# Reordering the start of the second attention of a two-layer decode kernel on Trainium2

## The chip, the cores and the metric

The kernel runs on one core of a Trainium2 chip. The metric is the device time of one execution in microseconds (us), median of several runs. All times inside an execution are counted from the start of the profiled span.

## The reference

```python
def _A_ref(x, k_cache, v_cache, wq, wo):            # x: 4 x 1 x 512, caches: 4 x 8 x 8192 x 128
    W = 2048                                        # the last 2048 rows of the caches
    q = (x @ wq) as 4 x 32 heads x 1 x 128
    k, v = last W rows, each of 8 KV heads serves 4 query heads
    p = softmax(q k^T * 128**-0.5)
    return (p v as 4 x 1 x 4096) @ wo
def _B_ref(x, w_gate, w_up, w_down):                # 512 -> 1792 -> 512
    return (sigmoid(x @ w_gate) * (x @ w_up)) @ w_down

x = x + _A_ref(layernorm(x)); x = x + _B_ref(layernorm(x))
x = x + _A_ref(layernorm(x)); x = x + _B_ref(layernorm(x))    # same weights and caches again
```

Everything is bf16 outside; there are four tokens (one per batch element), so every weight and every cache row is read for very little arithmetic.

## The kernel before

**One planner, five queues.** The Python functions below record operations with `P.op(engine, name, planned duration, emit, r=, w=, banks=)`. `_schedule` then orders each engine's operations by planned times; the order is fixed when the program is built, and each engine works through its list strictly in that order. Reads, writes and PSUM banks decide which semaphores an operation waits for. After the first layer `P.chain` is set: TensorE then follows the order in which the operations were recorded.

**Memory.** `arena` has 50 slots of 512 KB (a tile is two slots, 1 MB). Sixteen tiles hold K of all eight KV heads (`kpair(h, bp)`, two tiles for each head, `bp` picks two of the four batch elements); the rest circulate among wq, wo, V, gate, up and down. K is loaded once and stays, transposed in place, for the second attention. V is loaded twice, except that two V tiles are kept: one stays in the arena, the other is copied by VectorE into PSUM banks 0 to 3 at the end of the first attention (`stash`, operations `st0` to `st3`) and copied back in the second (`load_stash`, operations `us0` to `us3`, L517). The copies back may run once the first q of the second attention is turned (`fresh`).

**DMAs.** All weights and caches go through SyncE's queue at L398, in the order of the list `loads`. A load is recorded when a tile becomes free (`done` or `pool.release`, then `fill`); its DMA waits for the last reader of the tile's old content, and all later DMAs of the queue stand behind it.

**The second attention** (`attn_second`) works heads 7 to 0 as units 0 to 7. In each unit:

- `qx(u)`: TensorE spreads q (L721), ScalarE copies it to `qbd` (L726);
- `score(u)`: four mask matmuls (L751) and 16 score matmuls (L758) into one PSUM bank; then both K tiles of that head are released, which records the next V loads;
- `soft(u)`: on VectorE the maximum `mx` (L767), two copies (L771), `mk` (L775) and `nm` (L779); on ScalarE the exponential (L782), which writes `prow`;
- `turn(u)`: TensorE permutes `prow` (L795, PSUM bank 2), ScalarE copies it back (L797), VectorE transposes it to `ebuf` (L802);
- `sum_up(u)` (POOL L891, L898, L908; TensorE L903; VectorE L905), `pv_wide` (L925, then VectorE L933, L938, L940), and the output projection (L959, L965, L978). Unit 7 takes an older path (`pv_unit`, L844).

q comes in two halves. `q_second` makes the half for heads 4 to 7. The half for heads 0 to 3 is made inside `attn_second` from two wq tiles by `q_mms(1, 0, ...)` (L674), and turned by `q_turn` (VectorE L687, L691).

Before the change the recorded order at the top of `attn_second` is: spread q for unit 0; the first two quarters of the other q half; spread q for unit 1; score 0; score 1; softmax 0; turn 0; spread q for unit 2; the last two quarters of q; sums 0; turn of q; softmax 1. The stashed V returns to the tile that the first of those two wq tiles leaves.

**The last GLU** (`glu(1, 0, NB, True)`): gate matmuls and up matmuls (L1174, four chunks `c` each), VectorE transposes (L1183) and the gating (L1189 to L1201), then the down matmuls (L1214), which add to rows of x that `x_rows` (POOL L1149, TensorE L1156) has put into the same PSUM bank. ScalarE and VectorE copy the sum out (L1225) and SyncE stores it.

Of the kernel before, what the change touches and what calls it, by code (L numbers as in the profile page):

```python
# [278 lines left out]
def build(nc, A_x, A_k, A_v, A_wq, A_wo, B_wg, B_wu, B_wd, out, cfg=None):  # L279
    cfg = dict(cfg or {})  # L280
    tm = dict(_TM)
# [40 lines left out]
    with es:  # L322
# [188 lines left out]
        def load_stash(name):  # L511
            left[name] = 1

            def emit(s):
                for n, b in [(n, STASH[n]) for n in (1, 2, 3, 0)]:
                    dst = tile_ap(s)[:, n * 1024:(n + 1) * 1024].bitcast(F32)
                    o = P.op("vector", "us%d" % n, c_dve(512), lambda v, dst=dst, b=b: v.transpose(dst, ps[:, b, :]),  # L517
                             r=[("stash", n)], w=[("slot", s + n // 2)], banks=(b,))
                    o.deps.update(fresh)
            loads.append((name, emit))  # L520
# [219 lines left out]
        def softmax_unit(tag, hk, wait=False, q=True):  # L740
            u = ucount[0]
            ucount[0] += 1
            k2 = u % 2
            bank, pt = {HKV: (OBS[0], 2), HKV + 1: (WB, 3)}.get(u, (SB[k2], k2))
            if q:
                q_unit(tag, hk, k2)

            def e_s(pe):
                last = None
                for gi in range(4):  # L750
                    last = pe.matmul(ps[32 * gi:32 * gi + 32, bank, :], msk_s[:, :],  # L751
                                     msk_m[:, :].unsqueeze(1).broadcast_to([128, 256, 2]), start=True, stop=False)
                for cp in range(4):
                    for gi in range(4):
                        jh, bp = gi // 2, gi % 2
                        kt = kpair(hk, bp).rearrange("p (j c k t) -> p c t j k", c=2, k=32, t=2)
                        q0 = ((k2 * 4 + cp) * 2 + bp) * 32
                        last = pe.matmul(ps[32 * gi:32 * gi + 32, bank, :], qbd[:, q0:q0 + 32],  # L758
                                         kt[:, cp // 2, cp % 2, jh * NJ:(jh + 1) * NJ, :], start=False, stop=(cp == 3))
                return last  # L760
            P.op("tensor", "S" + tag, 20 * tm["pe_row"], e_s,
                 r=[("msk_s",), ("msk_m",)] + [("slot", 4 * hk + t) for t in range(4)] + [("q", k2)],
                 w=[("pss", pt)], banks=(bank,))
            def soft():
                mk = mxt[:, k2 * 32:(k2 + 1) * 32]
                P.op("vector", "mx" + tag, c_dve(512),
                     lambda v: v.tensor_reduce(nmax[:, k2:k2 + 1], ps[:, bank, :], AXX, ALU.max),  # L767
                     r=[("pss", pt)], w=[("mx", k2)], banks=(bank,))
                for g in range(2):
                    P.op("vector", "nx%d%s" % (g, tag), tm["dve_small"],  # L770
                         lambda v, g=g: v.tensor_copy(nmax[64 * g:64 * g + 64, 4 + k2:5 + k2],  # L771
                                                      nmax[64 - 64 * g:128 - 64 * g, k2:k2 + 1]),
                         r=[("mx", k2)], w=[("nx", k2, g)])
                P.op("vector", "mk" + tag, tm["dve_small"],
                     lambda v: v.scalar_tensor_tensor(mk, nmax[:, 4 + k2:5 + k2].broadcast_to([128, 32]), nmax[:, k2:k2 + 1],  # L775
                                                      maskr[:, :], ALU.max, ALU.add),
                     r=[("mx", k2), ("nx", k2, 0), ("nx", k2, 1), ("maskr",)], w=[("mk", k2)])
                P.op("vector", "nm" + tag, tm["dve_small"],
                     lambda v: v.tensor_reduce(nmax[:, 2 + k2:3 + k2], mk, AXX, ALU.max, negate=True, apply_transpose=True),  # L779
                     r=[("mk", k2)], w=[("nm", k2)])  # L780
                P.op("scalar", "ex" + tag, c_act(512) + 200.0,
                     lambda a: a.activation(prow[:, :].rearrange("p (m x t) -> p m x t", x=32, t=2),  # L782
                                            ps[:, bank, :].rearrange("p (m t x) -> p m x t", x=32, t=2), ACTF.Exp, bias=nmax[:, 2 + k2:3 + k2], scale=1.0,
                                            accum_out=psm[:, k2:k2 + 1]),
                     r=[("pss", pt)] + [("nm", k2)], w=[("prow",), ("psm", k2)], banks=(bank,))

            if wait:
                late[tag] = soft
            else:
                soft()  # L790
            return k2
# [260 lines left out]
        def attn_second():  # L1052
            hs = list(range(HKV))[::-1]

            def tag(u):
                return "2.%d" % u

            def turn(u):
                turn_p(2, tag(u), u % 2, PBS[0], u < NW)

            def qx(u):
                if u < HKV:
                    q_unit(tag(u), hs[u], u % 2)

            def score(u):
                if u >= HKV:
                    return
                softmax_unit(tag(u), hs[u], True, False)
                for bp in range(2):
                    pool.release(4 * hs[u] + 2 * bp)  # L1070
                fill()

            def soft(u):
                if u < HKV:
                    late.pop(tag(u))()

            def sum_up(u):
                if u < NW:
                    sums(tag(u), u % 2)
                elif u < HKV:  # L1080
                    sums_old(tag(u), u % 2)

            qx(0)
            q_mms(1, 0, OBS[1], (0, 1))
            qx(1)
            score(0)
            score(1)
            soft(0)
            turn(0)
            qx(2)  # L1090
            s = need(wq_part(1, NC - 1, 0)[0])
            left[wq_part(1, NC - 1, 0)[0]] += 1
            q_mms(1, 0, OBS[1], (2, 3))
            wide_buffers(s, P.ops[-1])
            sum_up(0)
            q_turn(1, 0, OBS[1], rest["tv", 1], [("tv", 1)], [o for o in P.ops if o.name == "pt2.0"])
            soft(1)
            op = {}

            def wo(u):  # L1100
                wo_wide(tag(u), hs[u], op[u], u % 2, u == 0, u == NW - 2)

            def back(u):
                op[u] = late.pop(("tr", tag(u)))()

            for u in range(NW):
                if u == NW - 1:
                    back(u - 1)
                    wo(u - 1)
                pv_wide(tag(u), hs[u], u % 2, v_tiles[(2, hs[u])])  # L1110
                turn(u + 1)
                if 0 < u < NW - 1:
                    back(u - 1)
                score(u + 2)
                soft(u + 2)
                if u == NW - 1:
                    wo_back()
                sum_up(u + 1)
                qx(u + 3)
                if 0 < u < NW - 1:  # L1120
                    wo(u - 1)
            u = NW

            def between():
                wo_compact(tag(u - 1), hs[u - 1], late.pop(("tr", tag(u - 1)))(), (u - 1) % 2)
            wo_unit(tag(u), hs[u], pv_unit(tag(u), hs[u], u % 2, v_tiles[(2, hs[u])], between), u % 2, False, True)
# [10 lines left out]
        def glu(k, b0, b1, last=False):  # L1137
# [24 lines left out]
            egv = eg[:, 0:NH].rearrange("p (k b) -> p k b", b=NB)  # L1162
            for n, nm in enumerate(("wg", "wu")):
                for c in range(NC):
                    if n and c == 2 and last:
                        x_rows()
                    name = (nm, c // 2, k)
                    s = need(name)

                    def e_g(pe, c=c, s=s, n=n):  # L1170
                        last = None
                        for g in range(4):
                            o = c % 2 * F + g * NF
                            last = pe.matmul(ps[32 * g:32 * g + NB, OBS[n], 0:NF], xn[:, c * NB:(c + 1) * NB],  # L1174
                                             tile_ap(s)[:, o:o + NF], start=(c == 0), stop=(c == NC - 1))
                        return last
                    P.op("tensor", "gl%s%d_%d" % (nm, k, c), 4 * tm["pe_row"], e_g,
                         r=tok(s) + [("xn",)], w=[("gu", n)], banks=(OBS[n],))
                    done(name)
# [7 lines left out]
                if n == 0:  # L1187
# [13 lines left out]
                 lambda v: v.tensor_tensor(hT[:, 0:NH].rearrange("p (k b) -> p k b", b=NB), tv, egv, ALU.mult),  # L1201
                 r=[("e", 0), ("e", 1), ("eg",), ("q", 0)], w=[("hT",)])
            if last:
                for (a, b) in bounds_of(k):
                    name = ("wd", a, k)
                    s = need(name)
# [157 lines left out]
```

## Time and profile before

| | us |
|---|---|
| median of 6 runs | 183.9 (183.42 to 184.71) |
| the profiled execution: its own time | 184.37 |
| the profiled execution: its span | 182.6 |
| TensorE busy | 100.2 (55%) |
| VectorE busy | 102.0 (56%) |
| ScalarE busy | 32.9 (18%) |
| POOL busy | 21.4 (12%) |
| SyncE's DMA queue: 71.84 MB, share of 16 engines | 96.4% |
| HBM read | 71.83 MB, 393 GB/s over the span |

Busy shares are averages over stages that differ: in the first attention VectorE transposes K, in the second it doesn't. The page's slices cut the span into 40 parts of 4.57 us. The second attention begins near 126 us and ends near 170 us, the last GLU after it.

### The profile page before, as it was taken

How to read it: one execution, taken by the hardware profiler on the slowest of the kernel's cores; microseconds unless marked ns; L12 is line 12 of the kernel's file. 1: busy time of each engine (PE TensorE's matmuls, PEld its weight loads, DVE VectorE, ACT ScalarE, POOL GpSimd, SP SyncE). 2: the span in 40 equal slices, each digit the busy share in tenths (PEclk: the TensorE clock that was granted, in tenths of full speed). 3: DMA queues.
4: the chain of work that ended last, by engine and by line, in shares of the span. 5: the costliest groups of instructions: out<-in, count | busy, mean ns of one | idle time of the engine just before them, and what ended most of it. 6: DMA issues, size and time to landing. Idle time of an engine off the chain costs nothing.

```text
span 182.6 us, 3840 instructions
## 1 busy us (share of the span) xinstructions
PE 100.2 (55%) x1627; PEld 54.1 (30%) x1639; DVE 102.0 (56%) x253; ACT 32.9 (18%) x87; POOL 21.4 (12%) x86
## 2 busy tenths in 40 slices
PE   1434425662816508254186566445866978757663
PEld 1002111342412504224146531321323333326331
DVE  6208997668384393744942633212978587743351
ACT  2002032121210202102002001001154244331011
POOL 7000010110010100101001000000024133322000
PEclk9999999999999999999999999999999699999555
DMA  5999999999999999999999999999999999999970
GB/s 198 420 425 429 425 414 417 422 420 414 418 416 425 423 422 413 422 416 423 407 423 418 410 402 414 357 371 387 416 357 414 427 427 418 423 406 408 412 312 16
DMA packets 12305, 72.09 MB, mean 395 GB/s; under 512 B 1144, under 2 KB 1152, under 8 KB 5632
## 3 DMA queue, kind: packets, MB, share of 16 engines
q1 hardware_dynamic: 12280, 71.84, 96.4%
q8 instruction: 13, 0.21, 0.5%
q14 instruction: 4, 0.03, 0.0%
q10 hardware_dynamic: 8, 0.00, 0.0%
HBM read 71.83 MB, written 0.00 MB: 393 GB/s over the span
## 4 chain that ended last, share of the span: by engine, by line
DMA 37%; DVE 27%; PE 23%; ACT 4%; SPq 3%; issue 3%; POOL 0%; DVEq 0%; ACTq 0%
DMA arena<-in_A_v_cache_dram 19%; DMA arena<-in_B_w_down_dram 12%; DVE arena L733 11%; PE ps L758 9%; DMA arena<-in_A_wq_dram 5%; PE ps L844 5%; DVE nmax L767 4%; SPq L398 3%; PE ps L751 3%; ACT prow L782 3%; DVE nmax L771 2%; DVE mxt L775 2%; DVE arena L933 1%; PE ps L1024 1%; DVE arena L517 1%
## 5 line engine op out<-in xcount | busy, mean ns | idle before, releaser
L733 DVE STREAM_TRANSPOSE arena<-arena 128x1024 f32<-128x1024 f32 x32 | 37.0, 1203 | 0.0
L758 PE MATMUL ps<-arena,qbd 128*32 128x512 bf16 x256 | 26.0, 541 | 0.0
L844 PE MATMUL ps<-ebuf,arena 128*128 128x8 bf16 x576 | 17.8, 168 | 9.4 <-DMA arena<-in_A_v_cache_dram 5.3
L767 DVE TENSOR_REDUCE nmax<-ps 128x1 f32<-128x512 f32 x16 | 11.0, 687 | 18.3 <-PE ps L758 18.3
L751 PE MATMUL ps<-msk_m,msk_s 128*32 128x512 bf16 x64 | 8.7, 532 | 22.0 <-DVE arena L733 21.8
L844 PEld LDWEIGHTS ps<-ebuf,arena 128*128 128x128 bf16 x576 | 16.8, 104 | 11.5 <-DMA arena<-in_A_v_cache_dram 6.4
L782 ACT ACTIVATE prow<-ps,nmax 128x512 bf16<-128x512 f32 x16 | 11.0, 687 | 37.5 <-DVE nmax L779 34.8
L726 ACT CAST qbd<-ps 128x256 bf16<-128x256 f32 x16 | 6.0, 373 | 47.1 <-PE ps L758 34.7
L674 PE MATMUL ps<-arena,xn 128*4 128x512 bf16 x64 | 7.9, 577 | 8.4 <-DMA arena<-in_A_wq_dram 7.3
L758 PEld LDWEIGHTS ps<-arena,qbd 128*32 128x32 bf16 x256 | 8.7, 123 | 10.4 <-issue 8.3
L811 POOL CAST s<-psm 128x1 bf16<-128x1 f32 x9 | 1.7, 189 | 84.5 <-ACT prow L782 84.0
L797 ACT CAST prow<-ps 128x512 bf16<-128x512 f32 x16 | 9.4, 586 | 10.8 <-PE ps L795 2.8
L802 DVE STREAM_TRANSPOSE ebuf<-prow 128x256 f32<-128x256 f32 x16 | 7.0, 439 | 4.7 <-ACT prow L797 4.6
L687 DVE STREAM_TRANSPOSE ebuf<-ps 128x512 f32<-128x512 f32 x3 | 2.2, 717 | 12.7 <-PE ps L674 12.6
L721 PE MATMUL ps<-qh,eyew 32*128 32x64 bf16 x64 | 5.7, 220 | 5.6 <-ACT qbd L726 2.4
L751 PEld LDWEIGHTS ps<-msk_m,msk_s 128*32 128x32 bf16 x64 | 1.8, 101 | 23.4 <-DVE arena L733 19.0
L655 ACT ACTIVATE lnv<-ps 128x4 f32<-128x4 f32 x4 | 0.7, 174 | 42.7 <-PE ps L651 42.7
L1174 PE MATMUL ps<-arena,xn 128*4 128x448 bf16 x64 | 7.0, 564 | 2.5 <-DMA arena<-in_B_w_up_dram 1.8
L852 DVE TENSOR_TENSOR onb<-ps,rinv 128x16 bf16<-128x16 f32 x9 | 1.7, 186 | 10.7 <-PE ps L844 10.7
L925 PE MATMUL ps<-arena,ebuf 128*32 128x512 bf16 x112 | 7.5, 389 | 0.0
L933 DVE STREAM_TRANSPOSE arena<-ps 128x512 f32<-128x512 f32 x7 | 5.0, 708 | 3.3 <-PE ps L925 3.3
L795 PEld LDWEIGHTS ps<-prow,perm 128*128 128x128 bf16 x16 | 1.6, 100 | 16.8 <-ACT prow L782 16.0
(105 smaller groups left out, 127.6 us busy)
## 6 DMA issues: line engine op xcount, KB each, us to landing
arena<-in_A_v_cache_dram SPq DMA_DIRECT2D x30, 1024.0 KB, 20.5
arena<-in_A_k_cache_dram SPq DMA_DIRECT2D x16, 1024.0 KB, 25.2
arena<-in_A_wq_dram SPq DMA_DIRECT2D x8, 1024.0 KB, 9.6
arena<-in_A_wo_dram SPq DMA_DIRECT2D x4, 1024.0 KB, 25.0
arena<-in_B_w_gate_dram SPq DMA_DIRECT2D x4, 896.0 KB, 16.8
arena<-in_B_w_up_dram SPq DMA_DIRECT2D x4, 896.0 KB, 16.3
arena<-in_B_w_down_dram SPq DMA_DIRECT2D x2, 1024.0 KB, 13.2
arena<-in_B_w_down_dram SPq DMA_DIRECT2D x1, 768.0 KB, 7.5
```

Source lines behind the costliest of these rows:

```text
L674: last = pe.matmul(ps[32 * hh:32 * hh + NB, qb, :], xn[:, c * NB:(c + 1) * NB], tile_ap(s)[:, o + hh * 512:o + (hh + 1) * 512], start=(c = ...
L733: P.op("vector", "T%d_%d" % (h, t), c_dve(1024), lambda v, v32=v32: v.transpose(v32, v32), r=[("slot", 4 * h + t)], w=[("slot", 4 * h + t)])
L751: last = pe.matmul(ps[32 * gi:32 * gi + 32, bank, :], msk_s[:, :], msk_m[:, :].unsqueeze(1).broadcast_to([128, 256, 2]), start=True, stop= ...
L758: last = pe.matmul(ps[32 * gi:32 * gi + 32, bank, :], qbd[:, q0:q0 + 32], kt[:, cp // 2, cp % 2, jh * NJ:(jh + 1) * NJ, :], start=False, s ...
L767: lambda v: v.tensor_reduce(nmax[:, k2:k2 + 1], ps[:, bank, :], AXX, ALU.max),
L782: lambda a: a.activation(prow[:, :].rearrange("p (m x t) -> p m x t", x=32, t=2), ps[:, bank, :].rearrange("p (m t x) -> p m x t", x=32, t ...
L797: P.op("scalar", "pc" + tag, c_act(512), lambda a: a.copy(prow[:, :], ps[:, pb, :]), r=[("ppb", pb)], w=[("prow",)], banks=(pb,))
L802: P.op("vector", "pt" + tag, c_dve(256), lambda v: v.transpose(et, prow[:, :].bitcast(F32)), r=[("prow",)], w=[("e", k2)])
L844: last = pe.matmul(ps[:, ob, bp * 8:bp * 8 + 8], src[:, j * 128:(j + 1) * 128], ev[:, j % 2, j % 16 // 2, x0:x0 + 8], start=(j == 0), stop ...
L925: last = pe.matmul(ps[32 * g:32 * g + 32, ob, :], ew[:, g, mq, t], src.rearrange("p (m t d) -> p t m d", t=2, d=128)[:, t], start=(n == 0) ...
L933: P.op("vector", "tv" + tag, c_dve(512), lambda v: v.transpose(tv, ps[:, ob, :]), r=[("pso", k2, 0), ("pso", k2, 1)], w=[("tv", k2)], bank ...
L1174: last = pe.matmul(ps[32 * g:32 * g + NB, OBS[n], 0:NF], xn[:, c * NB:(c + 1) * NB], tile_ap(s)[:, o:o + NF], start=(c == 0), stop=(c == N ...
```

## The change

Four edits:

1. In `attn_second` score 0 now comes directly after the first spreading of q, ahead of both quarters of q and of the spreading for unit 1, and softmax 0 is recorded inside `score(0)`, ahead of the release of the K tiles. The spreading for unit 1 stands ahead of the two quarters of q.
2. In the second attention the four mask matmuls of a score become an operation of their own, recorded just ahead of the score and without its wait for q.
3. Since score 0 now releases its K tiles first, the stashed V returns to the first K tile of head 7; the copies back are issued in the order 2, 1, 3, 0 instead of 1, 2, 3, 0.
4. In the last GLU `x_rows` is recorded after the up matmuls and the gating instead of between the second and the third chunk of up.

```diff
             def emit(s):
-                for n, b in [(n, STASH[n]) for n in (1, 2, 3, 0)]:
+                for n, b in [(n, STASH[n]) for n in (2, 1, 3, 0)]:
...
-            def e_s(pe):
+            def e_m(pe):
                 last = None
                 for gi in range(4):
                     last = pe.matmul(ps[32 * gi:32 * gi + 32, bank, :], msk_s[:, :],
                                      msk_m[:, :].unsqueeze(1).broadcast_to([128, 256, 2]), start=True, stop=False)
+                return last
+
+            def e_s(pe):
+                last = None if wait else e_m(pe)
                 for cp in range(4):
...
-            P.op("tensor", "S" + tag, 20 * tm["pe_row"], e_s,
+            if wait:
+                P.op("tensor", "M" + tag, 4 * tm["pe_row"], e_m, r=[("msk_s",), ("msk_m",)], w=[("pss", pt)], banks=(bank,))
+            P.op("tensor", "S" + tag, (16 if wait else 20) * tm["pe_row"], e_s,
...
                 softmax_unit(tag(u), hs[u], True, False)
+                if u == 0:
+                    soft(0)
                 for bp in range(2):
                     pool.release(4 * hs[u] + 2 * bp)
                 fill()
...
             qx(0)
+            score(0)
+            qx(1)
             q_mms(1, 0, OBS[1], (0, 1))
-            qx(1)
-            score(0)
             score(1)
-            soft(0)
             turn(0)
...
                 for c in range(NC):
-                    if n and c == 2 and last:
-                        x_rows()
                     name = (nm, c // 2, k)
...
             if last:
+                x_rows()
                 for (a, b) in bounds_of(k):
```

## The prediction

> **What bounds the kernel now.** I read the page's slices first, then the stretches around the changed place, then the timeline there and at the end.
>
> ```profile
> PEclk9999999999999999999999999999999699999555
> DMA  5999999999999999999999999999999999999970
> GB/s 198 420 425 429 425 414 417 422 420 414 418 416 425 423 422 413 422 416 423 407 423 418 410 402 414 357 371 387 416 357 414 427 427 418 423 406 408 412 312 16
> ```
>
> The 16 DMA engines are busy until the last slices: the weight stream carries the kernel. It runs near 420 GB/s, but at 357 to 387 between 114 and 128 us and again at 357 in slice 29 (132 to 137 us), just behind the changed place. The stretches (elapsed us, busy us and count of PE, PEld, DVE, ACT, POOL, clock, DMA share, GB/s) resolve that slice:
>
> ```profile
> 132.00:133.00 1.00, 0.00 (x0) 0.00 (x0) 0.93 (x4) 0.78 (x2) 0.00 (x0) 1.00 0.96 320
> 133.00:134.00 1.00, 0.64 (x12) 0.36 (x13) 0.51 (x3) 0.54 (x2) 0.00 (x0) 1.00 0.98 360
> 134.00:135.00 1.00, 0.33 (x6) 0.15 (x2) 0.81 (x2) 0.76 (x3) 0.54 (x2) 1.00 0.88 352
> ```
>
> Against 420 the microseconds from 132 to 138 (320, 360, 352, 393, 385, 393) lack 0.75 us. The timeline (start, us, engine, line) shows why:
>
> ```profile
> 126.83 0.37 ACT L726 CAST qbd<-ps 128x256 bf16<-128x256 f32 x1 [3.11 <-PE ps L721]
> 126.87 1.02 PE L674 MATMUL ps<-arena,xn 128*4 128x512 bf16 x8
> ...
> 127.95 2.66 DVE L517 STREAM_TRANSPOSE arena<-ps 128x512 f32<-128x512 f32 x4 [1.66 <-PE ps L674]
> ...
> 128.55 1.92 PE L758 MATMUL ps<-arena,qbd 128*32 128x512 bf16 x16
> ...
> 130.52 13.71 SPq L398 DMA_DIRECT2D arena<-in_A_v_cache_dram  x12
> ...
> 132.03 0.65 DVE L767 TENSOR_REDUCE nmax<-ps 128x1 f32<-128x512 f32 x1
> ...
> 134.56 0.69 ACT L782 ACTIVATE prow<-ps,nmax 128x512 bf16<-128x512 f32 x1 [0.24 <-DVE ebuf L802]
> ...
> 136.04 0.39 PE L795 MATMUL ps<-prow,perm 128*128 128x512 bf16 x1
> ...
> 137.95 0.65 DVE L767 TENSOR_REDUCE nmax<-ps 128x1 f32<-128x512 f32 x1
> ```
>
> The third V load starts at 130.52, when score 0 has let go of K. The load before it went out at 125.20 and landed 9.1 us later, at 134.3; the third lands 7.2 us after its issue, at 137.7. Between them lie 3.4 us, where 1 MB at 420 GB/s takes 2.5. Further on the queue is deep (the first down load is issued at 157.56 and lands at 177.7), so no later issue is short of time. The end:
>
> ```profile
> 177.03 0.22 DVE L1201 TENSOR_TENSOR hT<-ebuf,qbd 128x56 bf16<-128x56 f32 x1
> 177.67 1.02 PE L1214 MATMUL ps<-arena,hT 128*4 128x128 bf16 x32 [1.37 <-DMA arena<-in_B_w_down_dram]
> 178.93 1.02 PE L1214 MATMUL ps<-arena,hT 128*4 128x128 bf16 x24 [0.23 <-DMA arena<-in_B_w_down_dram]
> ```
>
> The down matmuls wait for their three loads (177.7, 178.9, 179.5) and end at 179.97. But hT is ready at 177.25; 56 matmuls at their pace here (8 in 0.41 with the drain, 32 in 1.02) need 1.9 us, so with the weights present they would end at 179.2. The stream leads the arithmetic by only 0.8 us. Both must be followed.
>
> **What the skill says.** The Trainium skill, "TensorE: Matmul & The Clock Gate", section "What's actually happening", has TensorE at half clock until it was busy for a free-running window of about 3.4 us. The trace agrees in kind: 16 score matmuls take 1.92 us at 128.55 and 1.11 at 136.59. At 128.55 the granted clock nevertheless reads 1.00, so I go by durations. "Perfetto Trace Analysis", section "Tensor Engine Instruction (MATMUL, LD_WEIGHTS)", calls ScalarE and VectorE strict FIFO and matmul ends modelled; nothing in this timeline overtakes. "DMA: Bandwidth & Descriptors", section "Anatomy of one DMA — SWDGE (gpsimd) path", puts the fixed part of a DMA near 2 us; the shortest issue to landing here, 4.9 us less 2.5 of movement, is similar.
>
> **Score 0 first (edit 1) with masks ahead (edit 2).** Spreading q ends at 126.80; the copy to qbd ends at 127.20. The four masks (0.40 us, from 128.15 to 128.55) fit into that wait and cost nothing; without this cover they would cost 0.40. Score 0 runs from 127.25 to 129.17 instead of ending at 130.47. The third V load goes out 1.3 us earlier. The fourth now waits for the q quarters: spreading for unit 1 (0.39), eight L674 matmuls (1.02), about 130.5 instead of 131.10. The fifth waits for score 1: masks and score behind that, about 131.8 to 132.3 instead of 131.85. SyncE issues the same DMAs in the same order. The later loads wait for PV 0, score 2 and on, where the queue is deep again (the load issued at 136.15 lands 11.8 us later). Gain for the stream: between 0 (the low rate has another cause) and the full 0.75; I take 0.7.
>
> For masks of units 2 to 7 the changed program keeps the place: behind L795 and L959, just before their score. Nothing, between -0.33 each (were they covered) and +0.05 each for one more semaphore update; I take 0.
>
> **VectorE's queue (edits 1 and 3).** This is the step that decides. Before, VectorE's list is: four copies of V back (2.66 us, 127.95 to 130.61, while TensorE makes the scores), mx to nm of unit 0, mx to nm of unit 1 (132.03 to 133.58), then the transpose L802 and the turn of q. In the changed program mx 0 comes first, the copies follow nm 0, and mx 1 stands behind the turn of q. So:
>
> - mx 0 waits for score 0: 129.20. VectorE idles from 126.29 to there, 2.9 us instead of 1.66. mx to nm takes 1.58 (130.53 to 132.11): 130.78.
> - copies 2.66: 133.44. ScalarE's exponential 0 ends at 131.7, L795 and L797 at 132.8, so L802 (0.45) follows at once: 133.92.
> - L905 (0.16), L687 (0.72), L691 (0.27), with gaps of 0.03: 135.15. L905 needs L903 on TensorE, due about 133.85: no wait, if score 1 runs at the fast clock.
> - mx to nm of unit 1, 1.55: 136.7. Exponential 1 (0.69 and 0.19 for the sum) ends at 137.65. It began at 134.56 before.
> - L795 of unit 1 stands in TensorE's list ahead of masks and score 2. Before it came at 136.04, after PV 0; now at 137.70. From there to the end of score 2 are 1.66 us (136.04 to 137.70): 139.36. mx 2 starts at 139.39 instead of 137.95: **1.4 us later**.
>
> From mx 2 on the units repeat every 4.29 us (143.05, 147.33, 151.62) through mx, nm, exponential, L795, masks, score, and no V is late for them, so the 1.4 us run through to the last GLU.
>
> Order 2, 1, 3, 0 frees bank 2 for L795 first: 131.4, before the exponential's 131.7. The old order would have cost up to 0.4 there, but nothing behind it, since VectorE is the later one. The other tile for V changes which reader is waited for (score 0, already waited for): 0.
>
> **x rows (edit 4).** The up chunks start at 174.21; the third at 175.33, 1.12 later, where two chunks need 0.92. Taking L1156 from between them is worth 0.2 if the second up load is there (153.21 plus 22.0: 175.2, so today almost 0). Behind up it runs while VectorE makes hT (0.9 us) and costs nothing; with no cover it would cost its 0.65.
>
> **Sum.** hT: 177.25 + 1.4 - 0.2 = 178.45. Down matmuls 1.9: 180.4 against 179.97, plus 0.4. The stream alone would end 0.7 earlier, at 179.3: no longer the bound. On the profiled execution 184.37 + 0.4 = 184.8. That execution lies 0.47 above the median; where the weights land that much earlier, the arithmetic is the bound already, and the loss is 0.9 on 183.9: again **184.8**. A measurement of this kernel tells about 0.5% (0.92 us) from no change; the forecast lies at that edge.
>
> **Rivals.**
> - *The stream still decides.* The low slices speak for it. It needs 1.1 us of the delay to vanish: the last three slices run at half clock (PEclk 5), and if the half-clock stretch fell elsewhere, gate, up and down (1.66, 1.88, 1.9 us) would shorten by about half. Then the end is 0.7 earlier: 183.7 on the profile, 183.2 on the median: not slower. It decides as soon as hT is ready before 177.4. Against it: nothing in the change moves that stretch.
> - *TensorE stays slow through score 1.* Then score 1 costs 0.8 more, L903 comes about 135.1 and VectorE idles 1.1 before L905: delay 2.5, end 185.9.
> - *Nothing of it reaches the end:* the slow stretch at 141 to 144 us (slice 31, PEclk 6), which doubles score 3 (1.93 against 1.11), falls beside it now, returning 0.8. Then 184.0.
>
> **Numbers.** VectorE's queue, 184.3 to 185.5: 0.55; the stream: 0.2; slow score 1: 0.13; nothing: 0.12. The likeliest case straddles the 0.5% edge at 184.82. A stream gain beyond 0.75 with a faster tail gives the faster share. Range 183.0 to 186.0. Faster 0.15, same 0.42, slower 0.43.
>
> **What would show it.** Right: L758 of unit 0 ends near 129.2, the V loads start there, slice 29 returns to about 415 GB/s, L517 runs after 130.7, the second L782 near 136.7, hT near 178.4, and no L1214 waits for a DMA. Wrong: mx 2 before 138.5 (the queue argument fails), or L1214 still waiting for its last load.

## The result, and the profile after

| | before | changed |
|---|---|---|
| median of the runs taken together, us | 184.17 (183.42 to 185.44) | 184.42 (183.2 to 185.59) |
| ratio changed / before, 95% interval | | 1.0005 [0.999, 1.002] |
| the profiled execution: own time, span, us | 184.37, 182.6 | 184.57, 182.8 |

The ratio is not the quotient of the two medians; comparisons below go by the ratio and its interval. There is no difference that this measurement can tell. Yet almost nothing in the second half of the execution is where it was. In the changed kernel's listing the lines of the scores, softmax and turns stand 4 to 6 further down: L758 is L762, L767 is L773, L782 is L788, L795 is L801, L802 is L808, L925 is L931, L1201 is L1206, L1214 is L1220.

The slices of the changed kernel:

```profile
PEclk9999999999999999999999999999996999996658
GB/s 193 418 428 430 425 413 422 418 418 414 418 419 425 421 416 415 426 416 419 413 422 416 411 405 418 356 375 391 410 421 425 421 421 419 421 408 404 418 232 9
```

The hole in the stream behind the changed place is closed (slice 29: 421 GB/s, 357 before). The half-clock slices have moved: before, slice 31 and the last three read 6 and 5; now slice 30 and slices 36 to 38 do, and the last one reads 8. The timeline of the changed kernel around the changed place (start, us, engine, line):

```profile
127.16 1.90 PE L762 MATMUL ps<-arena,qbd 128*32 128x512 bf16 x16
...
129.10 12.12 SPq L398 DMA_DIRECT2D arena<-in_A_v_cache_dram  x8
...
130.62 2.47 DVE L517 STREAM_TRANSPOSE arena<-ps 128x512 f32<-128x512 f32 x4
...
134.68 0.68 DVE L773 TENSOR_REDUCE nmax<-ps 128x1 f32<-128x512 f32 x1
...
136.29 0.69 ACT L788 ACTIVATE prow<-ps,nmax 128x512 bf16<-128x512 f32 x1 [3.44 <-DVE nmax L785]
...
137.12 0.61 PE L801 MATMUL ps<-prow,perm 128*128 128x512 bf16 x1 [2.49 <-ACT prow L788]
...
138.06 1.92 PE L762 MATMUL ps<-arena,qbd 128*32 128x512 bf16 x16
...
140.04 0.69 DVE L773 TENSOR_REDUCE nmax<-ps 128x1 f32<-128x512 f32 x1 [1.21 <-PE ps L762]
```

Score 0 ends at 129.06 and the V loads start at 129.10: 1.4 us earlier than before. VectorE's list is the forecast one: mx 0, nm 0, the four copies, L808, the turn of q, and only then mx 1, at 134.68 (132.03 before). Unit 1's L801 comes at 137.12 (136.04), and score 2 then takes 1.92 us (1.11 before), because a half-clock stretch has come to lie on it; mx 2 is 2.1 us later than before. Before, that stretch lay on score 3. From mx 3 on (144.31 against 143.05) every unit is 1.23 to 1.26 us later than before. The end:

```profile
164.40 1.92 PE L931 MATMUL ps<-arena,ebuf 128*32 128x512 bf16 x16
...
178.85 0.22 DVE L1206 TENSOR_TENSOR hT<-ebuf,qbd 128x56 bf16<-128x56 f32 x1
...
179.21 0.95 PE L1220 MATMUL ps<-arena,hT 128*4 128x128 bf16 x56 [1.03 <-DVE hT L1206]
```

No L1220 waits for a DMA now. The last down load is on chip at 179.20 in the slowest of the 16 DMA engines (179.52 before) and at 176.62 in the median one (177.52). hT is ready at 179.07 (177.25 before), 56 matmuls take 0.95 us instead of the 1.9 forecast, and they end at 180.16 against 179.97. The chain of waits, the work that ended last followed back, says the same. The last of its long pieces (start, us, what), first of the kernel before, then of the changed one:

```profile
163.09 15.79 DMA arena<-in_B_w_down_dram
```

```profile
179.21 0.98 PE ps L1220 x56
```

Before, the last long piece is a down load, with two short groups of down matmuls and the output behind it; now the pieces from 163 us on are arithmetic alone. In these two executions the bound has changed hands, at nearly the same time.

### The profile page after: what moved, and what is told of

Its sections match the earlier page's. It is cut to its first block, busy times and chain, and to the rows that moved or that the text cites. A ratio compares the mean times of both kernels' runs of the same rounds, so it can differ in the third digit from the quotient of the medians.

```text
span 182.8 us, 3839 instructions
## 1 busy us (share of the span) xinstructions
PE 99.3 (54%) x1627; PEld 53.9 (29%) x1639; DVE 101.5 (55%) x253; ACT 32.9 (18%) x87; POOL 21.4 (12%) x86
## 4 chain that ended last, share of the span: by engine, by line
DMA 33%; DVE 28%; PE 26%; ACT 4%; SPq 3%; issue 3%; POOL 0%; DVEq 0%; ACTq 0%
DMA arena<-in_A_v_cache_dram 23%; PE ps L762 9%; DVE arena L733 9%; DMA arena<-in_A_wq_dram 5%; DMA arena<-in_B_w_up_dram 5%; DVE nmax L773 5%; PE ps L850 4%; SPq L398 3%; PE ps L751 3%; ACT prow L788 3%; DVE nmax L777 2%; DVE mxt L781 2%; PE ps L1030 1%; DVE arena L939 1%; PE ps L1179 1%
## 5 line engine op out<-in xcount | busy, mean ns | idle before, releaser
L762 PE MATMUL ps<-arena,qbd 128*32 128x512 bf16 x256 | 25.8, 539 | 0.0
L773 DVE TENSOR_REDUCE nmax<-ps 128x1 f32<-128x512 f32 x16 | 11.1, 691 | 21.9 <-PE ps L762 21.9
L788 ACT ACTIVATE prow<-ps,nmax 128x512 bf16<-128x512 f32 x16 | 11.0, 687 | 38.1 <-DVE nmax L785 35.6
L762 PEld LDWEIGHTS ps<-arena,qbd 128*32 128x32 bf16 x256 | 8.4, 121 | 10.4 <-issue 7.8
L808 DVE STREAM_TRANSPOSE ebuf<-prow 128x256 f32<-128x256 f32 x16 | 7.0, 437 | 5.6 <-ACT prow L803 5.5
L931 PE MATMUL ps<-arena,ebuf 128*32 128x512 bf16 x112 | 8.2, 416 | 0.0
L801 PEld LDWEIGHTS ps<-prow,perm 128*128 128x128 bf16 x16 | 1.6, 101 | 19.4 <-ACT prow L788 18.5
```

The costliest lines, as they stand in the source:

```text
L808: P.op("vector", "pt" + tag, c_dve(256), lambda v: v.transpose(et, prow[:, :].bitcast(F32)), r=[("prow",)], w=[("e", k2)])
L931: last = pe.matmul(ps[32 * g:32 * g + 32, ob, :], ew[:, g, mq, t], src.rearrange("p (m t d) -> p t m d", t=2, d=128)[:, t], start=(n == 0) ...
```

## The experiments

Two things are to be told apart: does the arithmetic now set the end (and through which step), or the stream; and what are the half-clock stretches worth, of which the prediction took one for fixed. Orders of single operations were changed by added dependencies ahead of the planner's call:

```
named = dict((o.name, o) for o in P.ops)
for late_op, first_op in [...]:
    named[late_op].deps.add(named[first_op])
```

In these names `mx2.1` is mx of unit 1, `S2.1` its score, `us0` to `us3` the copies of V, `nm2.1` nm of unit 1, `pt2.0` L808 of unit 0, `qc1_0` the end of the turn of q (L691). Where a profiled time is compared with a median, the execution's own time is given.

**mx 1 late, in the kernel before** (`('mx2.1', 'qc1_0')`): nothing of the change but its late mx 1.

> The kernel before, with the maximum of unit 1 (mx 1) held in VectorE's list behind the turn of q, nothing else changed. Theory A, the arithmetic decides the end once it is later: exponential 1 starts near 137.3 instead of 134.56, mx 2 near 139.9 instead of 137.95 (2.0 later), hT 2.0 later, and the time rises by 1.0 to 1.5 us (0.5 to 0.8%). Theory B, the weight stream decides: the same traces up to hT, but the end stays within 0.3 us of before.

186.33 us, ratio 1.0100 [1.0069, 1.0130]. Its mx of units 1 and 2 in the timeline:

```profile
135.75 0.69 DVE L767 TENSOR_REDUCE nmax<-ps 128x1 f32<-128x512 f32 x1
...
141.12 0.69 DVE L767 TENSOR_REDUCE nmax<-ps 128x1 f32<-128x512 f32 x1 [1.21 <-PE ps L758]
```

mx 2 comes 3.2 us later than before, and the down matmuls wait for hT (ready at 182.60) and for no DMA, the last load being on chip at 179.7. So the place of mx 1 does reach the end, and VectorE's queue can decide it. By the ratio the price is 1.8 us, above the expected 1.0 to 1.5, though the interval reaches down to 1.3. This execution's own time is 188.11, so its times are read for their order and not for sizes; it ran at half clock from 137.16 to 150.81.

**Third V load late, first attempt** (`("('V', 6, 1, 1)", 'S2.1')`).

> The changed kernel, with the third V load of the second attention held until score 1 has ended (near 131.3 instead of 129.1), VectorE's list as in the changed kernel. Theory A: slice 29 falls back to about 350 to 380 GB/s, the stream's last load lands up to 1 us later, mx 2 and hT stay, and the time stays within 0.3 us of the changed kernel, since the arithmetic sets its end. Theory B: the time rises by 0.7 to 0.9 us.

A miss: the operation named there is the first V load of the second attention and not the third, so all of them stood behind score 1 and the queue ran empty (slices 27 and 28 at 106 and 161 GB/s). 188.54 us, ratio 1.0232 [1.0205, 1.0259]; the last load landed at 184.74 and the down matmuls waited for it. It shows only that a stream held up by some 5.5 us sets the end.

**Copies of V split around mx 1** (the copies as 2, 0, 1, 3, the last two and the turn of q behind L808, PV 0 behind score 2):

```
-for n, b in [(n, STASH[n]) for n in (2, 1, 3, 0)]:
+for n, b in [(n, STASH[n]) for n in (2, 0, 1, 3)]:
 ...
+[('mx2.1', 'us0'), ('pt2.0', 'nm2.1'), ('us1', 'pt2.0'), ('us3', 'us1'), ('ri2.0', 'us3'), ('qt1_0', 'ri2.0')]
```

> The changed kernel, with VectorE's list reordered: two of the four copies of V back before mx to nm of unit 1, then L808, then the other two copies and the turn of q; PV of unit 0 is moved behind score 2 on TensorE. mx 2 should start near 136.7, against 140.0 in the changed kernel and 137.95 before. Theory A: with the stream's gain now uncovered, the end is the stream's, 0.5 to 0.9 us below before (183.3 to 183.7). If the change gained nothing in the stream: no more than 0.2 us below before.

**mx 1 ahead of the turn, in the changed kernel** (`('mx2.1', 'us0'), ('pt2.0', 'nm2.1')`): the four copies, then mx 1 to nm 1, then L808 and the turn of q.

> The changed kernel with only one thing different: mx to nm of unit 1 stand ahead of L808 and the turn of q in VectorE's list (still behind all four copies). Exponential 1 should start near 135.2 instead of 136.3, mx 2 near 138.2 to 139. Theory A: the arithmetic ends about 1 us earlier than in the changed kernel, the time falls by 0.3 to 0.8 us against it. Theory B (stream): no difference from the changed kernel.

183.98 us, 0.9992 [0.9973, 1.0012], for the split copies; 183.97, 0.9995 [0.9976, 1.0013], for mx 1 first. Both bring mx 1 forward again (132.28 and 132.96; mx 2 at 137.55 and 138.65) and neither is measurably under the kernel before or under the changed kernel, so the expected falls did not show in either. For the split copies this is the result that was expected if the stream had gained nothing; their profile shows another reason, given below. By the second interval mx 1 first is at most 0.4 us under the kernel before, so no more than that of the stream's gain reaches the end there. With mx 1 first, in the profiled execution, hT is ready at 177.02 and the down matmuls wait again. Its timeline:

```profile
176.80 0.22 DVE L1206 TENSOR_TENSOR hT<-ebuf,qbd 128x56 bf16<-128x56 f32 x1
...
178.68 0.10 PEld L1220 LDWEIGHTS ps<-arena,hT 128*4 128x4 bf16 x8 [0.32 <-DMA arena<-in_B_w_down_dram]
```

The split copies lost their gain to the clock: half clock from 141.07 to 147.90 us (mx 7 at 161.85, 1.6 us later than before) and again from 164.96 to 178.62, hT at 179.56, arithmetic last.

**Third V load late, properly** (`("('V', 5, 1, 1)", 'S2.1')`), once in the changed kernel (with `('mx2.1', 'qc1_0')`, which keeps its order) and once in the version with mx 1 first. All engines keep their order in both.

> The changed kernel with the third V load of the second attention held until score 1 (it was free behind score 0), and mx 1 kept where it is, so that every engine has the changed kernel's order. The load goes out about 2.5 us later. Theory A (the arithmetic is the bound of the changed kernel, the stream just behind): the later loads land up to 0.8 us later, near 179.5 to 180, still about when the down matmuls want them; 184.4 to 184.9. Theory B (the stream sets the end in the changed kernel too, so that its gain is what kept the time): the whole 0.8 us returns, 185.2 or more. Theory C (the earlier load gave the stream nothing that reaches the end): 184.4 as the changed kernel, and the last load lands when it did.

> The version with mx 1 ahead of the copies (x4) with the third V load held until score 1, all engines' orders as in x4. There the last load set the end (178.64 against hT at 177.0). Theory A and B: the stream lands 0.4 to 0.8 us later and the end with it: 184.4 to 184.8 against 184.0 of x4. Theory C (the earlier V load is worth nothing at the end): 184.0 again.

185.13 us, 1.0033 [1.0013, 1.0053], and 185.06 us, 1.0043 [1.0027, 1.0060]. With mx 1 first, the two ratios (1.0043 against 0.9995) lie apart by 0.48%, 0.9 us, and the intervals do not touch. The load goes out at 131.35 instead of 128.87 (130.52 in the kernel before), the loads behind it 1.3 to 1.8 us later, slice 29 falls to 339 GB/s, and the last down load lands at 177.53 (median engine) and 180.77 (slowest) instead of 176.52 and 178.64; the down matmuls wait for it, and the chain ends with a piece `DMA arena<-in_B_w_down_dram`. So the time of the third V load reaches the end where the stream is the bound. The size is not the change's own: this edit moves the load by 2.5 us, 0.8 beyond its place in the kernel before, while the change moved it by 1.4. What those 1.4 us are worth at the end was not run by itself. In the changed kernel the same edit costs about 0.5 us (1.0033 against 1.0005, intervals that just overlap). There the load goes out only at 132.96, and its profiled execution (185.87) is bound by the arithmetic (hT at 179.81, last load 180.07), and score 1 ran at half pace (1.92 us); how much of the 0.5 is stream stays open.

**x rows alone** (the kernel before with edit 4 only).

> The kernel before with the x rows alone moved behind the up matmuls. Theory A: hT up to 0.2 us earlier, but the down matmuls wait for their loads there, so the time stays: 184.1 to 184.3. Rival: the x rows stood on the path that sets the end and cost their 0.65: 183.6.

184.24 us, 0.9997 [0.9981, 1.0012]. hT is ready at 177.03, and the down matmuls wait for their loads at 177.63 and 178.87 as before. That hT is 0.2 us earlier is not shown to come from the edit: this execution had no half-clock stretch between 132.64 and 166.78, gate started 1.1 us earlier than before (171.04 against 172.10), and then the third up chunk waited 1.09 us for its load and started at 175.16. What the x rows cost by themselves was hidden there, and the time is the same.

**Old order of the stashed copies** (the changed kernel with `(1, 2, 3, 0)`).

> The changed kernel with the old order of the stashed V copies (banks 1, 2, 3, 0). Theory A: L801 of unit 0 comes up to 0.4 us later and VectorE, behind its copies, is late by that or by nothing: 184.4 to 184.7. Rival (the order is what paid for the loss elsewhere): 185 or more.

184.15 us, 0.9995 [0.9977, 1.0012]; mx 1 at 134.76 (134.68), unit 1's L801 at 137.20 (137.12). The order of the copies is worth nothing that can be seen. The other half of edit 3 (the tile that V returns to) and edit 2 were not run alone; what they are worth is not shown.

**TensorE kept busy.** The traces so far let one look at the half-clock stretches. Windows of the changed kernel, 3.41 us each, cut so that its changes of clock fall on their edges (elapsed us, busy us and count of PE, PEld, DVE, ACT, POOL, granted clock, DMA share, GB/s):

```profile
160.59:164.00 3.41, 1.52 (x24) 0.54 (x16) 1.98 (x7) 0.95 (x5) 0.92 (x3) 1.00 0.99 404
164.00:167.41 3.41, 3.06 (x25) 1.76 (x26) 1.00 (x2) 1.09 (x2) 0.72 (x4) 0.50 1.02 403
167.41:170.83 3.42, 2.71 (x82) 2.53 (x83) 0.87 (x4) 0.26 (x2) 1.16 (x3) 1.00 1.04 410
170.83:174.24 3.41, 1.83 (x37) 1.48 (x33) 1.19 (x7) 0.00 (x0) 0.00 (x0) 0.50 1.02 411
174.24:177.65 3.41, 3.29 (x34) 1.40 (x38) 1.38 (x6) 0.72 (x4) 0.00 (x0) 0.50 0.60 239
177.65:181.07 3.42, 1.48 (x72) 0.93 (x64) 1.88 (x6) 0.51 (x2) 0.00 (x0) 1.00 0.08 28
```

Each row's clock fits the PE column of the row above it: 1.52 us busy, then half; 3.06, then full; 2.71, then half; 1.83, then half; 3.29, then full. But a pair of rows of the kernel before does not fit:

```profile
171.73:175.14 3.41, 3.06 (x35) 1.30 (x34) 1.48 (x6) 0.60 (x4) 0.00 (x0) 0.50 1.01 412
175.14:178.55 3.41, 2.04 (x48) 0.97 (x40) 1.59 (x4) 0.12 (x1) 0.00 (x0) 0.50 0.58 231
```

Here the same 3.06 us busy at half clock were followed by half clock. The last section comes back to this. To test whether a busier TensorE gets full clock, mask matmuls whose result nobody reads were put where TensorE waits:

```
+pe.matmul(ps[32 * gj:32 * gj + 32, bank, :], msk_s[:, :],
+          msk_m[:, :].unsqueeze(1).broadcast_to([128, 256, 2]), start=True, stop=True)
```

In the head, 9, 8 and 11 of them in the waits between 119.5 and 126.3 us, ahead of score 0 (bank WB); in the tail, 42 in seven waits from 162 us on (bank 0).

> The changed kernel with 42 mask matmuls (0.10 us each at full clock) into a PSUM bank that nobody reads any more, put where TensorE waits between 162 and 179 us (12, 4, 3, 4, 4, 7 and 8 of them), every other engine's order unchanged. In the traces so far a 3.41-us stretch at half clock followed one in which TensorE had been busy 0.3 to 0.8 of the time. Theory A (the loss of the changed kernel beyond VectorE's 1.2 us comes from those half-clock stretches, and the stream is 0.3 to 0.9 us earlier than before): the tail runs at full clock, hT comes 1 to 1.8 us earlier, near 177.4, the last load decides again: end of the down matmuls near 179.5, 183.7. Theory B (the stream alone decides the changed kernel): 184.4 as without. Rival C (the added matmuls only delay TensorE): 185 or more, and PEclk in the last slices stays 5 to 6.

> The changed kernel with 28 such matmuls where TensorE waits between 119.5 and 126.3 us (9, 8 and 11 of them, into a bank that is free there), ahead of score 0, which has run at half pace (1.90 us) in every trace. Theory A: TensorE has the full clock at 126.5, score 0 takes 1.1 us and ends 0.8 us earlier, near 128.3; third V load, mx 0 and the whole chain behind come 0.8 us earlier: hT near 178.1, 183.7 to 184.0. If the clock doesn't follow TensorE's busy share, score 0 takes 1.9 as before and the time is 184.4 to 184.9.

> The version with mx 1 ahead of the copies (x4) with both groups of added matmuls (28 ahead of score 0, 42 in the tail). Theory A: score 0 ends 0.8 us earlier, the tail is at full clock, hT near 175 and the down matmuls follow their loads alone: the end is the last landing plus 0.35 us, 178.3 to 179.0: 182.8 to 183.6. Theory B (the stream alone): 183.6 to 184.0, as x4. Rival C (added matmuls delay TensorE): 184.5 or more.

| | us | ratio to before |
|---|---|---|
| changed, busy tail | 184.08 | 1.0002 [0.9980, 1.0023] |
| changed, busy head | 183.80 | 0.9991 [0.9975, 1.0008] |
| mx 1 first, busy head and tail | 183.53 | 0.9974 [0.9959, 0.9989] |

The tail's matmuls kept the clock full through L931 (1.03 us) until 169.06, but from there to 179.30 it was half again, although TensorE was busy without a break from 169.06 to 172.47. hT came at 177.90, 1.2 us earlier than in the changed kernel, of which 0.65 was there at mx 7 already (160.79 against 161.44), ahead of the added matmuls. The end moved by 0.6 us in the profile (179.59), and the medians show no gain. That expectation failed. The head did what was expected and more; its timeline:

```profile
124.62 1.49 PE L1310 MATMUL ps<-msk_m,msk_s 128*32 128x512 bf16 x11
...
126.94 1.12 PE L762 MATMUL ps<-arena,qbd 128*32 128x512 bf16 x16
```

Score 0 takes 1.12 us instead of 1.90, mx 0 starts at 128.10, mx 2 at 138.29, hT is ready at 176.46: 2.6 us earlier than in the changed kernel and not the 0.8 expected, since later half-clock stretches moved too. By the ratios the time gains only 0.14%, 0.3 us, which the intervals do not tell from nothing. In the profile the loads take over: the last one lands at 178.90 in the slowest engine, and the down matmuls wait for it. With mx 1 first and both groups the end of the profiled execution is the landing and nothing else:

```profile
175.99 0.22 DVE L1206 TENSOR_TENSOR hT<-ebuf,qbd 128x56 bf16<-128x56 f32 x1
...
178.67 0.28 PE L1220 MATMUL ps<-arena,hT 128*4 128x128 bf16 x8 [0.23 <-DMA arena<-in_B_w_down_dram]
```

It is faster than the kernel before by 0.26% [0.11, 0.41], the only version that is, and by the ratios 0.3% under the changed kernel.

**The head's matmuls in the kernel before.**

> The kernel before with the 28 added matmuls ahead of its q spreading, nothing else changed. If the gain of the version with both groups (0.26%) comes from the full clock alone, without the change's order: 183.4 to 183.7. Theory A (the end is the later of the stream and the arithmetic, and the stream stays short of time between score 0 and the V loads unless score 0 comes first): score 0 ends 0.8 to 1.3 us earlier than 130.47, the third V load goes out near 129.4, slice 29 recovers about half, hT comes near 176.3, and the loads decide: 183.6 to 184.0.

184.21 us, 1.0004 [0.9975, 1.0033]. In its profile the full clock came only at 131.91, although TensorE was busy 0.97 and 0.90 of the two stretches of 3.41 us up to 128.50: score 0 still took 1.92 us and ended at 130.87. So it does not say what a fast score 0 would be worth without the change's order.

## Why the prediction was right, and where it was right by luck

The time was forecast at 184.8, a loss of 0.4 on the profiled execution and of 0.9 on the median known then; measured is a ratio of 1.0005, +0.1 us, inside the 0.5% that the prediction took as the least that can be told from no change. It held a loss that can be seen to be as likely (0.43) as none (0.42). The mechanism was the one it called likeliest, and the profile bears it out: the stream gains and is no longer the bound, VectorE's queue delays the arithmetic, and the arithmetic sets the end. By its own steps:

- **Score 0 and the stream.** Forecast: score 0 ends at 129.17, V loads at 129.2, gain 0.7. Measured: 129.06, 129.10; the last load is earlier by 0.9 us in the median engine, but by 0.3 in the slowest, and the down matmuls wait for all 16. The step took one number for a quantity that differs by engine: the 3.4 us that it read between the second and the third V landing are those of the slowest engine, in the median one they are 2.7. What the gain is worth at the end was not isolated; with mx 1 first it is at most 0.4 over many executions. The 2 us of fixed part that the prediction sets beside its shortest load are stated for DMAs that GpSimd issues; the loads here are SyncE's, and no step of the sum rested on it.
- **VectorE's queue.** Forecast delay 1.4, measured 1.23 at unit 7. Of this, mx 1's chain was quicker than forecast: the copies took 2.47 and not 2.66, exponential 1 started at 136.29, forecast just behind 136.7, L801 of unit 1 came at 137.12 and not 137.70. Then half clock on L801, the masks and score 2 cost 1.2 us that the forecast did not have (2.86 from L801 to the end of score 2, forecast 1.66), so that mx 2 came 2.1 us later than before and not 1.4 (140.04, forecast 139.39), and score 3 at full clock (1.08 us; 1.93 before) returned 0.8. That 1.4 and 1.23 lie so close is luck: two shifts of the clock nearly cancelled. The third rival had named just this return; it happened, only that the slow stretch moved onto score 2 and the return was spent there. The step also says that units repeat every 4.29 us from mx 2 on; in the kernel before mx 2 to mx 3 took 5.10 (137.95 to 143.05), because of that stretch.
- **"The 1.4 us run through to the last GLU."** About that much (1.23) ran to unit 7, and then it grew: half clock at 164.00 to 167.41 made L931 0.9 us longer, and unit 7's first PV came 2.3 us later than before (168.49 against 166.20). This step failed as a sum, since it treated the clock as fixed to the program.
- **Down matmuls 1.9.** They took 0.95, as full clock came back at 177.65. This term was mis-sized by about the same amount the other way, which is luck again. hT at 179.07 was forecast at 178.45; 0.6 too early there, 0.95 too late here: end 180.16 against 180.4.
- **Masks, stash order, x rows.** Costed at 0, 0 and 0.2 to hT. Masks: TensorE ran them at 126.63, in the wait for the q copy. The stash order: no effect that can be seen. x rows: in the changed kernel the up chunks run without a break, as forecast (16 matmuls in 1.49 us), but no run shows the 0.2 by itself; alone in the kernel before, the edit changes nothing at the end.
- **The rival "the stream still decides"** needed hT before 177.4. Against it stood "nothing in the change moves that stretch"; this was wrong, the stretches did move. It did not come about in the changed kernel's profile, but did as soon as mx 1 was put first.

So the near-zero result, as far as the profiles show it, is two effects on two paths that were 0.8 us apart: the stream got shorter (by 0.9 us in the median engine, by 0.3 in the slowest), the arithmetic longer by 1.0 (180.16 against the 179.2 that it could have reached before), and the end follows the later one. That each of the two paths can set the end is shown by the runs with mx 1 late and with the third V load late; the share of each in the change's own 0.1 us is argued from one profile. The clock shifts the arithmetic by a microsecond from case to case. That the spread of the changed kernel's runs (183.2 to 185.6) comes from those stretches too fits its profiles but was not shown run by run.

## What to carry to other kernels

Where two paths end within a microsecond of each other, shortening one shows nothing unless the other is kept from growing: follow both to the end, and look which of them ends the chain of waits in each version. Moving a wait ahead on one engine's list makes everything behind it late (here four copies and a turn of q ahead of the next maximum); after any reordering ask which short, critical operation now stands behind long, patient ones. And here, where TensorE waits much of the time, its clock depended on what it had just done: count matmul times from the trace at the place they will have, not where they were.

## What the runs showed of the hardware

- The Trainium skill, "TensorE: Matmul & The Clock Gate", section "What's actually happening", puts the return to half clock after an idle window of about 3.4 us. Here no such idle was needed. In the 14 profiled executions, cut into stretches of 3.41 us by the records of matmuls and clock, all 38 changes from full to half came right after a stretch in which TensorE was busy 0.08 to 0.79 of the time, and all 38 changes to full (14 of them the first entry of a record) after one of at least 0.80. The busy share is no rule all the same: the clock stayed at half after 19 stretches with a share of at least 0.80, two of them at 1.00, and stayed full after 78 with less than 0.80.
- The columns that matmuls streamed separate these stretches better. Count 512 for a matmul of `128x512`, 4 for one of `128x4`, from the same records. Of the 213 stretches behind the first entries of the records, all 117 with at least 11,800 columns were followed by full clock and all 76 with less than 10,250 by half clock; the 20 in between went either way. In the changed kernel 167.41 to 170.83 had 2.71 us busy but 562 columns, then half; with the busy tail 169.06 to 172.47 was busy throughout with 8,115 columns, then half. This was counted after the fact in the same traces. No run was made to test it, so what sets the clock stays open.
- The clock record begins at 129.87 in the changed kernel (130.77 before), and PEclk reads 9 ahead of it. The first attention's scores take 1.92 us each, as at half clock, so this 9 is no measurement, nor is the 1.00 that the prediction read at 128.55. With stretches counted back from its first entry, no trace has one of 11,800 columns earlier than the stretch right ahead of that entry (the largest is 11,720). The busy head, with full clock recorded from 126.78, brought a score 0 of 1.12 us.
- One load can land 3.7 us apart in the 16 DMA engines (changed kernel, last down load: 175.45 to 179.20, median 176.62), so a gain of the stream's mean is not the gain of its last landing.
